# Loading k in runs of four rows and turning all of q by DMA in a fused attention and feed-forward kernel

## The chip, the cores and the metric

The kernel runs on one core of one Trainium2 chip. The metric is the device time of one execution in microseconds; of the kernel before there are three runs. Engines are named as the profile names them: PE is TensorE (its weight loads are PEld), DVE is VectorE, ACT is ScalarE, POOL is GpSimd, and SP is SyncE, which here only issues DMAs.

## The reference

Eight batches of eight heads attend in a sliding window of 64 tokens; the result, with the heads side by side, goes through a feed-forward layer whose activation is h cos h.

```
q, k, v: (8, 8, 576, 64) float32     w_in: (512, 2048)     w_out: (2048, 512)

scores = (q @ k^T) / 8
mask   = (0 <= pos_q - pos_k < 64);   scores = where(mask, scores, -1e9)
attn   = softmax(scores)
x      = (attn @ v) as (8*576, 512)
h      = x @ w_in;   g = h * cos(h);   out = g @ w_out
```

## The kernel before

Everything that PE multiplies is bf16. The feed-forward part goes over nine tiles (mt) of 512 tokens. The first tile is written out by hand as a list of short names (FIRST), with the attention of batches 0 and 1. Each later tile has a first product (h_ps, 16 blocks of 128 columns of w_in, four matmuls each) and a second product (out_ps, four groups of 16 matmuls). After each of the 16 blocks ACT makes the sine (L595) and DVE multiplies it with h_ps into gT (L598), which frees the PSUM bank; h_ps takes turns in five banks. The second product reads all of gT.

The attention of the later batches is laid into these tiles by a plan: `at(time, fn, ...)` puts a step on it, and `pump(time)`, called after each block of the first product and after every four matmuls of the second, emits all steps that are due. One unit of this time is four matmuls of 512 columns, some 0.9 us; a tile has T = 32 units. The plan sets only the order in which instructions stand in each engine's queue. An engine takes its queue in order and waits at each instruction for what that one needs; an engine with nothing to wait for runs ahead of the plan.

Batch b is prepared in tile b - 1, which starts at t0 = T (b - 1):

- POOL issues the loads, which cast to bf16. `load_chunk` brings 96 tokens of all heads of q or k (six chunks each), `load_v` brings v.
- `turn_k` (L260) has SP issue a DMA transpose of each k chunk into kT, six per batch. `turn_q` (L244) does the same with q chunks into one tile `turned`, for as many chunks as TURNED tells: two in batches 4 to 6, six in batch 7. They are put on the plan about 6 to 9 units ahead of t0.
- The other q chunks are transposed on PE (`tr_q`, L219) and copied out of PSUM by DVE. From `turned` DVE copies as well (`put_turned`). Both write `qB`, in which each unit of 64 tokens stands as a block of 128 columns, one half for each head of a pair, zero elsewhere; so one matmul gives the scores of two heads.
- `g_scores` (L303) multiplies each unit with the keys of its own and the preceding 64 tokens (in the order that alternates from unit to unit). The groups of a batch start at t0 + 14.6, so just as the second product starts, and follow at 0.36 units per unit of work.
- `g_max` (DVE) adds the mask and finds the maximum, `g_exp` (ACT) takes exponentials and their sum, `g_inv` (DVE) the reciprocal, `g_norm` (POOL, L353) multiplies into w, and `g_trans` (SP, L367) has w turned by a DMA transpose into wT.
- `values` (L384) multiplies wT with v into the next tile's x, just ahead of that tile.

Stores of a tile's output are issued by SP too (L473), at the next tile's start.

Of the kernel before, what the change touches and what calls it, by code (L numbers as in the profile page):

```python
# [10 lines left out]
def _safe_warn(msg, *a, **kw):  # L11
# [3 lines left out]
F32 = mybir.dt.float32  # L15
BF16 = mybir.dt.bfloat16
# [7 lines left out]
NU = 9  # L24
# [18 lines left out]
DIRECT = (0, 7, 8)  # L43
OUTS = 3
FILL = (6, 12)
TURNED = {4: 2, 5: 2, 6: 2, 7: 6}

# [24 lines left out]
)  # L72


# [1 line left out]
def kernel(  # L76
# [59 lines left out]
    def copy(engine, out, in_):  # L136
        {"a": nc.scalar.copy, "p": nc.gpsimd.tensor_copy}.get(engine, nc.vector.tensor_copy)(out, in_)  # L137
# [17 lines left out]
            nc.scalar.copy(mask16[:, lo:hi], mask[:, of:of + hi - lo])  # L155


    def rows_tile(name):
        return ld.tile([128, NC * H * D], BF16, tag=name, name=name)

    def load_heads(name, b, p0=0, n=PAIRS):
        if (name, b) not in st:
# [90 lines left out]
    def k_tile(b):  # L253
        if ("kA", b) not in st:
            st["kA", b] = ka = att.tile([128, PAIRS, S], BF16, tag="kT", name="kT", bufs=2)
            st.update({("kT", b, p): ka[:, p] for p in range(PAIRS)})
        return st["kA", b]

    def turn_k(b, c):
        nc.sync.dma_start(out=k_tile(b)[:, :, c * NP:c * NP + NP], in_=st["k", b][:, c], transpose=True)  # L260

    def put_k(b, p, engine="a"):
        kt = k_tile(b)[:, p]
# [18 lines left out]
    def g_scores(n, which):  # L282
        s_ps = bank((BANKS if n < n_listed else S_BANKS)[which], "s_ps")
        units = groups[n]
        if n == FILL[1]:
            nc.tensor.matmul(out=s_ps, lhsT=ident, rhs=mask16[:, 0:4].rearrange("p u c -> p (u c)"), start=True, stop=True,
                             skip_group_check=True)
        s_ps = s_ps[:, 0:len(units) * 128].rearrange("p (u c) -> p u c", c=128)
        if n < n_first:
            m0 = 2 if units[0][2] else 0  # L290
            for h in range(2):
                d = slice(64 * h, 64 * h + 64)
                nc.tensor.matmul(out=s_ps[d].rearrange("p u c -> p (u c)"), lhsT=ident[d, d],
                                 rhs=mask16[d, m0:m0 + len(units)].rearrange("p u c -> p (u c)"),
                                 start=True, stop=False, skip_group_check=True)
        for u, (b, p, j) in enumerate(units):
            kt = st["kT", b, p]
# [4 lines left out]
            if b > 1:  # L302
                nc.tensor.matmul(out=s_ps[:, u, 0:64 * chunks].rearrange("p (a t) -> p a t", a=chunks),  # L303
                                 lhsT=qblocks[(b % 2) * PAIRS + p][:, j].rearrange("d h t -> d (h t)"), rhs=rhs,
                                 start=True, stop=True, skip_group_check=True)
                continue
            for h in range(2):
                d = slice(64 * h, 64 * h + 64)
                nc.tensor.matmul(out=s_ps[d, u, 0:64 * chunks].rearrange("p (a t) -> p a t", a=chunks),  # L309
                                 lhsT=qtiles[b * PAIRS + p][d, 64 * j:64 * j + 64], rhs=rhs[d], start=n >= n_first,  # L310
                                 stop=n >= n_first or u == len(units) - 1, skip_group_check=True)
        st["s", n] = s_ps


    def g_max(n):
        s_ps, units = st["s", n], groups[n]
        negm = att.tile([128, GF], F32, tag="negm", name="negm", bufs=8)
        if n < n_first:
            nc.vector.tensor_reduce(out=negm[:, 0:len(units)], in_=s_ps, op=ALU.max, axis=AX.X, negate=True)
        else:  # L320
            s = att.tile([128, GF, 128], F32, tag="s", name="s", bufs=4)
            for u, (b, p, j) in enumerate(units):
                c = slice(0, 128 if j else 64)
                nc.vector.tensor_tensor_reduce(out=s[:, u, c], in0=s_ps[:, u, c], in1=mask[:, 2 - j % 2 if j else 0, c],  # L324
                                               scale=-scale if b else -1.0, scalar=BIG, op0=ALU.add, op1=ALU.min,
                                               accum_out=negm[:, u:u + 1])
            st["s", n] = s
        st["m", n] = negm
# [11 lines left out]
    def g_inv(n):  # L340
        e, den = st["e", n]
        for u, (_, _, j) in enumerate(groups[n]):
            if j == 0 and n >= n_first:
                nc.vector.memset(e[:, u, 64:128], 0.0)
        rden = att.tile([128, GF], F32, tag="rden", name="rden", bufs=8)
        nc.vector.reciprocal(out=rden[:, 0:len(groups[n])], in_=den[:, 0:len(groups[n])])  # L346
        st["r", n] = rden

    def g_norm(n, engine="p"):
        (e, _), rden = st.pop(("e", n)), st.pop(("r", n))  # L350
        w = att.tile([128, GF, 128], BF16, tag="w", name="w", bufs=8)
        u = len(groups[n])
        (nc.gpsimd if engine == "p" else nc.vector).tensor_tensor(out=w[:, 0:u], in0=e[:, 0:u], op=ALU.mult,  # L353
                                in1=rden[:, 0:u].unsqueeze(2).to_broadcast([128, u, 128]))
        st["w", n] = w

    def g_trans(n):
# [119 lines left out]
    def at(time, fn, *args):  # L477
        plan.append((time, len(plan), fn, args))
# [11 lines left out]
    for t in range(1, B - 1):  # L490
        last = max(i for i, units in enumerate(groups) if units[0][0] == t + 1)
        time = T * t + Q - 1.4
        for i in range(last + 1 - n):
# [9 lines left out]
            ready.update({unit: time + (5.9 if n in direct else 8.5) for unit in groups[n]})  # L503
            n += 1

    for b in range(2, B):
        t0 = T * (b - 1)
        for h in range(2):
            if b in TURNED:
                at(t0 + 0.6 + 0.5 * h, put_turned, b, h, 0, 3)  # L510
            if TURNED.get(b, 0) > 2:
                at(t0 + (11 + h if TURNED[b] == NC else 10 + 0.5 * h), put_turned, b, h, 3, TURNED[b] * NP // 64)
        for c in range(TURNED.get(b, 0)):
            at(t0 - T + (24.3 if b == 4 else 23.4 if c < 2 else 26.4) + 0.01 * c, turn_q, b, c)
        for p in range(PAIRS if TURNED.get(b) != NC else 0):
# [12 lines left out]
        for half_ in range(2):  # L528
            at(t0 + ((24 if b == 3 else 22.2) + 0.1 * half_ if b > 2 else 10), spread_v, b, half_, "p" if b > 2 else "s")
# [18 lines left out]
    def spread_first(lo, hi):  # L548
# [6 lines left out]
             "Lv0": lambda c: load_v(0, c), "Lv1": lambda c: load_v(1, c), "Lq2": lambda c: load_chunk("q", 2, c), "Lk2": lambda c: load_chunk("k", 2, c),  # L555
# [93 lines left out]
```

## Time and profile before

| | |
|---|---|
| time, median of 3 runs | 309.44 us (308.31 to 310.33) |
| span of the profiled execution, first to last instruction | 306.3 us; the page gives no other time of this execution |
| PE busy | 296.2 us, 97% of the span |
| PEld, DVE, ACT, POOL busy | 52%, 75%, 76%, 63% |
| granted clock of PE | 1.000 |
| DMA moved | 42.14 MB in 159,945 packets, 148,256 of them under 512 bytes |
| POOL's DMA queue | 100,192 packets, 18.06 MB |
| queue of SP | 59,568 packets, 23.38 MB |
| DMA transposes issued by SP | 68 of wT, 36 of kT, 12 of qT |

Busy times are sums over one profiled execution and may overlap between engines. Matmuls are pipelined, so that PE's busy time holds time in which its pipe fills; how far apart two matmuls start tells what one costs. A line of the profile's tables gives the source line, the engine and the operation, output and inputs by the program's names, how often, busy time and the mean time of one, and the idle time before it with what ended it. A timeline gives start, duration, engine, line and operation, with the idle time before in brackets. For SP the time of an instruction is the time to issue a DMA, not to move its data; that is listed as "to landing", from the issue on.

### The profile page before, as it was taken

To read this page: it belongs to the slowest core of one execution; us is meant where nothing else is said; L and a number is where in the kernel's file an instruction comes from. 1 tells how busy PE (TensorE), PEld (TensorE's weight loads), DVE (VectorE), ACT (ScalarE), POOL (GpSimd) and SP (SyncE) were. 2 spreads that over 40 slices of the span, in tenths; PEclk is the share of its full clock that TensorE was granted. 3 is DMA by queue.
4 is the path that set the end of the run, shared out by engine and by line. 5 is a ranking of instruction groups with operands and counts; after the bars stand their busy time and mean duration, and the time that the engine had idled before them with its cause. 6 is when DMAs were issued, how large, how long until landed. Compare 5 with 4: busy or idle time off the path is not lost.

```text
span 306.3 us, 7904 instructions
## 1 busy us (share of the span) xinstructions
PE 296.2 (97%) x2616; PEld 159.0 (52%) x2616; DVE 228.5 (75%) x908; ACT 234.3 (76%) x785; POOL 192.5 (63%) x228
## 2 busy tenths in 40 slices
PE   3889999999999999999999999999999999999996
PEld 2768844545555555445544555454545554454443
DVE  5999978599769976798579857986698668235801
ACT  5998799677997799779976997699879986116600
POOL 8998579995659669967998599959903930000000
PEclk9999999999999999999999999999999999999999
DMA  7999999999999995999999999999794643011011
GB/s 146 179 212 192 200 180 130 121 149 191 226 113 116 175 223 80 121 133 232 125 121 137 231 143 104 157 221 148 86 137 107 169 78 141 2 68 71 1 67 70
DMA packets 159945, 42.14 MB, mean 138 GB/s; under 512 B 148256, under 2 KB 155168, under 8 KB 159904
## 3 DMA queue, kind: packets, MB, share of 16 engines
q0 software_dynamic: 100192, 18.06, 80.1%
q1 hardware_dynamic: 59568, 23.38, 40.6%
q8 instruction: 20, 0.33, 0.4%
q14 instruction: 21, 0.17, 0.2%
q10 hardware_dynamic: 144, 0.20, 0.2%
HBM read 36.70 MB, written 9.44 MB: 151 GB/s over the span
## 4 chain that ended last, share of the span: by engine, by line
PE 90%; POOL 4%; DMA 2%; DVE 1%; ACT 1%; issue 1%; POOLq 0%; DVEq 0%; ACTq 0%
PE h_ps L453 35%; PE out_ps L609 35%; PE h_ps L417 5%; PE s_ps L303 4%; PE out_ps L436 4%; PE o_ps L384 3%; DMA k<-in_k_dram 2%; POOL w L353 2%; PE tq_ps L219 1%; POOL v L188 1%; PE out_ps L465 1%; PE s_ps L309 1%; PE tw_ps L364 1%; POOL w_in L204 1%; ACT e L336 1%
## 5 line engine op out<-in xcount | busy, mean ns | idle before, releaser
L609 PE MATMUL out_ps<-w_out,gT 128*128 128x512 bf16 x496 | 117.3, 379 | 0.0
L453 PE MATMUL h_ps<-xT,w_in 128*128 128x512 bf16 x512 | 115.3, 379 | 0.3
L595 ACT ACTIVATE sin<-h_ps 128x512 f32<-128x512 f32 x128 | 73.7, 598 | 32.7 <-PE h_ps L453 31.4
L598 DVE TENSOR_TENSOR gT<-h_ps,sin 128x512 bf16<-128x512 f32 x128 | 82.1, 685 | 21.9 <-ACT sin L595 21.2
L336 ACT ACTIVATE e<-s,negm 128x128 f32<-128x128 f32 (+1 forms) x256 | 97.1, 382 | 0.6 <-DVE negm L324 0.6
L353 POOL TENSOR_TENSOR w<-e,rden 128x512 bf16<-128x512 f32 (+1 forms) x74 | 70.0, 962 | 36.6 <-DVE rden L346 18.8
L453 PEld LDWEIGHTS <-w_in 128*128 128x128 bf16 x512 | 48.8, 98 | 54.7 <-issue 0.4
L609 PEld LDWEIGHTS <-gT 128*128 128x128 bf16 x496 | 45.9, 98 | 44.2
L324 DVE CUSTOM_DVE_ANT_0 s<-s_ps,mask 128x128 f32<-128x128 f32 (+1 forms) x256 | 56.4, 279 | 1.7 <-PE s_ps L309 0.9
L336 ACT ACTIVATION_READ_ACCUMULATOR e<-s,negm 128x1 f32 x256 | 48.3, 189 | 0.0
L182 POOL DMA_DIRECT2D q<-in_q_dram x36 | 28.3, 785 | 10.7 <-DMA q<-in_q_dram 4.0
L188 POOL DMA_DIRECT2D v<-in_v_dram x40 | 34.4, 878 | 0.3 <-issue 0.2
L182 POOL DMA_DIRECT2D k<-in_k_dram x36 | 28.2, 783 | 3.9 <-DMA k<-in_k_dram 1.2
L137 ACT COPY out_sb<-out_ps 128x512 f32<-128x512 f32 (+1 forms) x18 | 10.2, 566 | 24.5 <-PE out_ps L609 18.4
L346 DVE RECIPROCAL rden<-den 128x4 f32<-128x4 f32 (+1 forms) x79 | 13.1, 166 | 19.0 <-ACT e L336 18.6
L303 PEld LDWEIGHTS <-qB 128*128 128x128 bf16 x216 | 16.5, 98 | 14.2
L137 DVE CAST xT<-o_ps 128x512 bf16<-128x512 f32 x24 | 15.5, 677 | 10.1 <-PE o_ps L384 10.1
L137 DVE COPY out_sb<-out_ps 128x512 f32<-128x512 f32 x18 | 12.4, 690 | 13.2 <-PE out_ps L609 12.5
L324 DVE DVE_READ_ACCUMULATOR2_ANT negm<- 128x1 f32 x256 | 21.3, 83 | 0.0
L303 PE MATMUL s_ps<-kT,qB 128*128 128x128 bf16 (+1 forms) x216 | 21.2, 216 | 0.0
L137 POOL COPY v<-v 64x1536 bf16<-64x1536 bf16 (+3 forms) x12 | 18.8, 1570 | 0.3
L137 DVE COPY qB<-tq_ps 64x384 bf16<-64x384 bf16 (+1 forms) x40 | 15.6, 390 | 0.4
(70 smaller groups left out, 257.8 us busy)
## 6 DMA issues: line engine op xcount, KB each, us to landing
out_dram<-out_sb SPq DMA_DIRECT2D x16, 512.0 KB, 7.5
v<-in_v_dram POOLq DMA_DIRECT2D x32, 128.0 KB, 5.7
q<-in_q_dram POOLq DMA_DIRECT2D x36, 96.0 KB, 8.6
k<-in_k_dram POOLq DMA_DIRECT2D x36, 96.0 KB, 8.5
w_in<-in_moe_w_in_dram POOLq DMA_DIRECT2D x4, 512.0 KB, 8.7
w_out<-in_moe_w_out_dram POOLq DMA_DIRECT2D x4, 512.0 KB, 10.8
wT<-w SPq DMA_TRANSPOSE x68, 4.4
q<-in_q_dram POOLq DMA_DIRECT2D x7, 144.0 KB, 6.0
```

Of the source, the lines that this page charges most:

```text
L137: {"a": nc.scalar.copy, "p": nc.gpsimd.tensor_copy}.get(engine, nc.vector.tensor_copy)(out, in_)
L182: nc.gpsimd.dma_start(out=st[name, b][:, c].rearrange("p (h d) -> p h d", h=H), in_=src.rearrange("h p d -> p h d"))
L188: nc.gpsimd.dma_start(out=vt.rearrange("p (h d) -> p h d", h=H), in_=v[b, :, c * 128:c * 128 + n, :].rearrange("h p d -> p h d"))
L303: nc.tensor.matmul(out=s_ps[:, u, 0:64 * chunks].rearrange("p (a t) -> p a t", a=chunks), lhsT=qblocks[(b % 2) * PAIRS + p][:, j].rearrang ...
L324: nc.vector.tensor_tensor_reduce(out=s[:, u, c], in0=s_ps[:, u, c], in1=mask[:, 2 - j % 2 if j else 0, c], scale=-scale if b else -1.0, sc ...
L336: nc.scalar.activation(e[:, u, c], s[:, u, c], AF.Exp, bias=negm[:, u:u + 1], scale=1.0 if n < n_first else -1.0, accum_out=den[:, u:u + 1])
L353: (nc.gpsimd if engine == "p" else nc.vector).tensor_tensor(out=w[:, 0:u], in0=e[:, 0:u], op=ALU.mult, in1=rden[:, 0:u].unsqueeze(2).to_br ...
L417: nc.tensor.matmul(out=h_ps[:, half * e:half * e + half], lhsT=w_in_sb[:, ks, ff * 128:ff * 128 + 128], rhs=st["xT", 0][:, ks, half * g:ha ...
L453: nc.tensor.matmul(out=st["h", ff], lhsT=w_in_sb[:, ks, ff * 128:ff * 128 + 128], rhs=st["xT", mt][:, ks], start=start, stop=stop)
L595: nc.scalar.activation(sin, h_ps, AF.Sin, bias=math.pi / 2.0)
L598: nc.vector.tensor_tensor(out=gt[:, e], in0=h_ps, in1=sin, op=ALU.mult)
L609: nc.tensor.matmul(out=o_ps[e], lhsT=gT[ff // 2][:, ff % 2, ms * 128:ms * 128 + 128], rhs=w_out_sb[:, ff], start=ff == 0, stop=ff == n_ff - 1)
```

## The change

k of batches 2 to 7 is loaded in one DMA for the first 512 tokens, with each partition holding four consecutive tokens of every head (runs of 1 KB), and one for the last 64 (`load_runs`, `load_rest`). DVE sorts the first into an order in which token 4p + c stands in part c at row p (`sort_runs`), and two DMA transposes, of 16 blocks and of four, make kT of it (`turn_runs`, `turn_rest`). So keys stand in kT by their place in the run of four, and the score matmuls read them in pieces of 16 columns (`keys_of`); a ninth unit needs two matmuls. The mask is sorted alike once, and `g_norm` brings the weights back into the order of v: it reads e in the sorted order and writes every fourth element. The reciprocal is written twice for this.

q of batches 3 to 7 is turned by DMA whole. Its transposes are put on the plan at t0 + 1.6 to t0 + 6.6, the copies into blocks at t0 + 6, 6.5, 11 and 12. They stand behind the two stores in SP's queue. `load_v` follows from batch 3 on at t0 + 8, as it did for batch 7.

```diff
-TURNED = {4: 2, 5: 2, 6: 2, 7: 6}
+TURNED = {3: 6, 4: 6, 5: 6, 6: 6, 7: 6}
+RUN = 4
...
+    def sort_masks():
+        for to in range(2):
+            copy("d", mask[:, to].rearrange("q (a c p) -> q a c p", a=2, c=RUN),
+                 mask[:, to + 1].rearrange("q (a p c) -> q a c p", a=2, c=RUN))
...
+    def load_runs(b, lo, hi):
+        if ("raw", b) not in st:
+            st["raw", b] = rows_tile("k")[:, 0:RUN * H * D].rearrange("p (h x) -> p h x", h=H)
+        nc.gpsimd.dma_start(out=st["raw", b][:, lo:hi],
+                            in_=k[b, lo:hi, 0:128 * RUN].rearrange("h (p c) d -> p h (c d)", c=RUN))
+
+    def load_rest(b):
+        st["rest", b] = rest = ld.tile([64, H * D], BF16, tag="rest", name="rest", bufs=1)
+        nc.gpsimd.dma_start(out=rest.rearrange("p (h d) -> p h d", h=H),
+                            in_=k[b, :, 128 * RUN:S].rearrange("h p d -> p h d"))
+
+    def sort_runs(b, engine=None):
+        st["sorted", b] = to = ld.tile([128, RUN * H * D], BF16, tag="sorted", name="sorted", bufs=1)
+        copy(engine, to.rearrange("p (c h d) -> p h c d", c=RUN, h=H),
+             st.pop(("raw", b)).rearrange("p h (c d) -> p h c d", c=RUN))
...
-    def turn_k(b, c):
-        nc.sync.dma_start(out=k_tile(b)[:, :, c * NP:c * NP + NP], in_=st["k", b][:, c], transpose=True)
+    def runs_of(b):
+        whole = k_tile(b).rearrange("d a s -> d (a s)")
+        return (whole[:, 0:128 * RUN * PAIRS].rearrange("d (c a p) -> d c a p", c=RUN, a=PAIRS),
+                whole[:, 128 * RUN * PAIRS:].rearrange("d (a t) -> d a t", a=PAIRS))
+
+    def turn_runs(b):
+        nc.sync.dma_start(out=runs_of(b)[0].rearrange("d c a p -> d (c a) p"), in_=st.pop(("sorted", b)), transpose=True)
+
+    def turn_rest(b):
+        nc.sync.dma_start(out=runs_of(b)[1], in_=st.pop(("rest", b)), transpose=True)
+
+    def keys_of(b, p, j):
+        runs, rest = runs_of(b)
+        n = 64 // RUN
+        if j == NU - 1:
+            return ((0, 1, rest[:, p].rearrange("d (p c) -> d c p", c=RUN).unsqueeze(1)),
+                    (1, 2, runs[:, :, p, n * j - n:n * j].unsqueeze(1)))
+        lo, chunks = max(n * j - n, 0), 2 if j else 1
+        keys = runs[:, :, p, lo:lo + n * chunks].rearrange("d c (a p) -> d a c p", a=chunks)
+        return ((0, chunks, keys[:, ::-1] if j and j % 2 == 0 else keys),)
...
+            multiply(out=w[:, 0:u].rearrange("q u (a p c) -> q (u a) c p", a=2, c=RUN),
+                     in0=e[:, 0:u].rearrange("q u (a c p) -> q (u a) c p", a=2, c=RUN), op=ALU.mult,
...
+    at(T + 4, sort_masks)
     for b in range(2, B):
         t0 = T * (b - 1)
-        for h in range(2):
-            if b in TURNED:
-                at(t0 + 0.6 + 0.5 * h, put_turned, b, h, 0, 3)
-            if TURNED.get(b, 0) > 2:
-                at(t0 + (11 + h if TURNED[b] == NC else 10 + 0.5 * h), put_turned, b, h, 3, TURNED[b] * NP // 64)
-        for c in range(TURNED.get(b, 0)):
-            at(t0 - T + (24.3 if b == 4 else 23.4 if c < 2 else 26.4) + 0.01 * c, turn_q, b, c)
+        if b in TURNED:
+            for c in range(NC):
+                at(t0 + 1.6 + c, turn_q, b, c)
+            for h in range(2):
+                at(t0 + 6 + 0.5 * h, put_turned, b, h, 0, 3)
+                at(t0 + 11 + h, put_turned, b, h, 3, NU)
...
         if b > 2:
+            at(t0 - T + 5.6, load_runs, b, 0, H)
+            at(t0 - T + 6.4, load_rest, b)
             for c in range(NC):
-                for i, name in enumerate(("q", "k")):
-                    at(t0 - T + 5.6 + 1.6 * c + 0.8 * i, load_chunk, name, b, c)
-        for c in range(NC):
-            at(t0 + (2 + 1.2 * c if b == 2 else (-5.4, -5.3, -5.2, -4, -2.5, -1.5)[c] if TURNED.get(b) == NC else c - 5.5),
-               turn_k, b, c)
+                at(t0 - T + 7.2 + 1.6 * c, load_chunk, "q", b, c)
+        at(t0 + (1.4 if b == 2 else -9.4), sort_runs, b)
+        at(t0 + (2 if b == 2 else -6.5), turn_runs, b)
+        at(t0 + (3.2 if b == 2 else -5.5), turn_rest, b)
```

More of the change, by code (lines that the diff above doesn't have):

```diff
@@ L296, in g_scores @@
         for u, (b, p, j) in enumerate(units):
+            if b > 1:
+                for a0, a1, keys in keys_of(b, p, j):
+                    nc.tensor.matmul(out=s_ps[:, u, 64 * a0:64 * a1].rearrange("p (a c t) -> p a c t", a=a1 - a0, c=RUN),
+                                     lhsT=qblocks[(b % 2) * PAIRS + p][:, j].rearrange("d h t -> d (h t)"), rhs=keys,
+                                     start=True, stop=True, skip_group_check=True)
+                continue
             kt = st["kT", b, p]
@@ L301, in g_scores @@
                 rhs = rhs[:, ::-1, :]
[L302 to L306, printed above, removed]
             for h in range(2):
@@ L323, in g_max @@
                 c = slice(0, 128 if j else 64)
-                nc.vector.tensor_tensor_reduce(out=s[:, u, c], in0=s_ps[:, u, c], in1=mask[:, 2 - j % 2 if j else 0, c],
+                nc.vector.tensor_tensor_reduce(out=s[:, u, c], in0=s_ps[:, u, c], in1=mask[:, 1 - j % 2 if b > 1 else 2 - j % 2 if j else 0, c],
                                                scale=-scale if b else -1.0, scalar=BIG, op0=ALU.add, op1=ALU.min,
@@ L344, in g_inv @@
                 nc.vector.memset(e[:, u, 64:128], 0.0)
-        rden = att.tile([128, GF], F32, tag="rden", name="rden", bufs=8)
-        nc.vector.reciprocal(out=rden[:, 0:len(groups[n])], in_=den[:, 0:len(groups[n])])
+        rden = att.tile([128, GF, 2], F32, tag="rden", name="rden", bufs=8)
+        u, twice = len(groups[n]), 2 if n >= n_listed else 1
+        nc.vector.reciprocal(out=rden[:, 0:u, 0:twice], in_=den[:, 0:u].unsqueeze(2).to_broadcast([128, u, twice]))
         st["r", n] = rden
@@ L352, in g_norm @@
         u = len(groups[n])
-        (nc.gpsimd if engine == "p" else nc.vector).tensor_tensor(out=w[:, 0:u], in0=e[:, 0:u], op=ALU.mult,
-                                in1=rden[:, 0:u].unsqueeze(2).to_broadcast([128, u, 128]))
+        multiply = (nc.gpsimd if engine == "p" else nc.vector).tensor_tensor
+        if n < n_listed:
+            multiply(out=w[:, 0:u], in0=e[:, 0:u], op=ALU.mult, in1=rden[:, 0:u, 0:1].to_broadcast([128, u, 128]))
+        else:
+            multiply(out=w[:, 0:u].rearrange("q u (a p c) -> q (u a) c p", a=2, c=RUN),
+                     in0=e[:, 0:u].rearrange("q u (a c p) -> q (u a) c p", a=2, c=RUN), op=ALU.mult,
+                     in1=rden[:, 0:u].rearrange("q u a -> q (u a)").unsqueeze(2).unsqueeze(3)
+                     .to_broadcast([128, 2 * u, RUN, 64 // RUN]))
         st["w", n] = w
@@ L504 @@
             n += 1
+    at(T + 4, sort_masks)
     for b in range(2, B):
         t0 = T * (b - 1)
[L508 to L515 removed]
+        if b in TURNED:
[4 more added lines that the diff above has]
+                at(t0 + 11 + h, put_turned, b, h, 3, NU)
+        for p in range(PAIRS if b not in TURNED else 0):
             t_q = t0 + (2 if b == 2 else 1) + (3.3 if b == 2 else 3.5) * p
```

4 lines of the change are left out of this document (2 added, 2 removed), and 6 rows, old and new, of the table FIRST.

## The prediction, made before the run

> **What bounds the kernel now.** I read the page's chain of waits first, to see which engine sets the end.
>
> ```profile
> PE 90%; POOL 4%; DMA 2%; DVE 1%; ACT 1%; issue 1%; POOLq 0%; DVEq 0%; ACTq 0%
> ```
>
> TensorE (PE) holds 90% of the chain, and what is not PE lies almost wholly before 60 us. After that PE runs without a gap, so a microsecond of PE work taken away is a microsecond won, and a microsecond in which PE has to wait is one lost. The change does something to both, once per tile of 512 tokens. So I next read the chain in order of time for one such period. Call P the start of a tile's first product (h_ps, L453); its score matmuls (s_ps) and second product (out_ps, L609) follow. Here are tile 4, where batch 5 is prepared, and tile 6, where batch 7 is prepared:
>
> ```profile
> 152.76 2.75 PE h_ps L453 x12
> ...
> 167.63 1.73 PE out_ps L609 x8
> ```
> ```profile
> 215.85 13.97 PE h_ps L453 x64
> 229.82 0.20 PE s_ps L303 x4
> ```
>
> In tile 6 all of q is turned by DMA already, and the 64 matmuls take 13.97 us, unbroken. In tile 4 sixteen PE transposes of q lie between them: the second product begins at 167.63 instead of 14.2 us after P, 0.7 us later. These are what the change takes away.
>
> What it adds is work for SP's queue, which issues every DMA transpose in order. So the third view is SP's own timeline around P = 152.76, with GpSimd's (POOL's) last normalisation beside it:
>
> ```profile
> 150.70 3.81 SPq L367 DMA_TRANSPOSE wT<-w  x3
> 154.60 2.51 SPq L260 DMA_TRANSPOSE kT<-k  x2
> 157.21 1.21 SPq L367 DMA_TRANSPOSE wT<-w  x1
> 158.51 1.21 SPq L260 DMA_TRANSPOSE kT<-k  x1
> 159.82 1.24 SPq L367 DMA_TRANSPOSE wT<-w  x1
> 161.15 2.52 SPq L260 DMA_TRANSPOSE kT<-k  x2
> 163.78 1.28 SPq L367 DMA_TRANSPOSE wT<-w  x1
> 165.15 2.21 SPq L260 DMA_TRANSPOSE kT<-k  x1
> 167.47 1.06 SPq L473 DMA_DIRECT2D out_dram<-out_sb  x2
> ```
> ```profile
> 153.47 1.04 POOL L353 TENSOR_TENSOR w<-e,rden 128x512 bf16<-128x512 f32 x1 [0.55 <-DVE rden L346]
> ```
>
> The reader is to see a backlog. The last weights (w) are ready at 154.5, yet SP issues their transpose at 163.78 and the stores at 167.47, because every issue takes it 1.2 us, 1.3 with the gap, and twelve stand in line from 150.70 on. Today no urgent work stands behind this line: q of batch 5 went out in front of it (two chunks from 147.22), and all six of batch 7 too:
>
> ```profile
> 217.51 5.25 SPq L244 DMA_TRANSPOSE qT<-q  x4
> ```
> ```profile
> 227.65 0.54 DVE L137 COPY qB<-qT 64x1536 bf16<-64x1536 bf16 x1
> ```
>
> The last four are issued from P+1.7 to P+5.6 and land by P+11.2; VectorE (DVE) copies them into blocks at P+11.8, and the first score matmul follows at P+13.97. The slack is 0.6 us. The last view is the time from issue to landing, in traffic (kT, in tile 4) and in a quiet stretch (two chunks of q):
>
> ```profile
> L260 SPq DMA_TRANSPOSE kT<-k x6: 1207/1211/2215, 154.6 to 165.1; - x6
> ...
> DMA to landing us min/median/max: 3.7/6.9/8.2
> ```
> ```profile
> L244 SPq DMA_TRANSPOSE qT<-q x2: 1207/1207/1207, 117.5 to 118.8; - x2
> ...
> DMA to landing us min/median/max: 2.3/2.3/2.3
> ```
>
> **The change, part by part.** *PE transposes of q (L219) leave tiles 2 to 5.* From the first h_ps to the first out_ps these tiles take 14.99, 14.71, 14.71 and 14.70 us; tile 6, without transposes, 14.01. The differences add up to 1.0 + 3 x 0.7 = 3.1 us saved: 72 transposes at 43 ns.
>
> *Score matmuls.* The ninth unit of a head pair is now two of 64 columns: 24 more. A 64-column one occupies 28 ns in the trace, a 128-column one 56; two halves equal one whole, so between 0 and 24 x 28 ns = 0.7 us. I take 0.7. Keys are now read in runs of 16 columns with a jump, and the last 64 at every fourth column. No row shows such a read; the nearest are the units that read their two chunks in reverse order, which cost the same 56 ns. I take nothing; the other end is half speed, 216 x 52 ns = 11.3 us (3.7% of the span). The Trainium skill's SBUF — State Buffer (section on the DMA port swizzle) says that strides up to 8 bf16 elements are free, since two accesses still share a 16-byte line. By it this price is nothing and the sum stays; no run here shows it yet.
>
> *k in runs.* Per batch six loads of 256-byte rows become one of 1 KB rows and a small one; POOL loses four issues of 0.78 us, which the chain doesn't see. Sorting is one DVE copy per batch of 2048 values: from 0.54 us for 1536 up to 1.12 us (the 64x2048 copy of v), among scores in the second product, where DVE has pauses of 0.6 to 0.8 us waiting for ACT: hidden, at worst 6 x 1.1. DVE loses 32 copies of q out of PSUM (0.35 to 0.45 us) and gains ten of 0.37 and 0.55; it comes out lighter in the first product.
>
> *The sorted normalisation on POOL* writes every fourth element. No row shows that either; between today's 1.04 us and, at half speed, 2.1. It stands ahead of SP's backlog, which is longer, so I take no cost.
>
> *The two k transposes.* The issue of 16 blocks instead of 4: transposes of three and four blocks both take 1.2 us, so I take 1.3 with the gap; the other end is in proportion, 4.8, which is 3.6 us more per period. In tile 1 the big one stands ahead of the sixth group's wT, which landed just at its use; its 2048 packets of 28 ns over 16 engines delay it by 0 to 3.6 us: 2 once.
>
> *q behind the backlog, the step that decides.* All six chunks of batches 3 to 7 are now emitted behind the two stores. For tile 4: the fifth wT can go at 149.6, when its w is ready; then the sixth wT, the runs, wT, the rest, three wT: eight issues x 1.3 = 10.4; stores 1.2. So the first chunk goes at 161.2 = P+8.4, the sixth 6.5 later, at P+14.9. The same count gives P+14.9 for tiles 5 and 6. In tiles 2 and 3, where fewer wT stand behind, the last w is ready at P+1.5 and P+1.7 and the sixth chunk goes at P+12.7. To these comes the landing. POOL loads the next batch in this stretch (before: from 154.45 for 15 us, much the same now), so I take 7 us, by the kT row; in tile 6, where only v is loaded, 3. Ends: 2.3 and 8.2.
>
> Behind the copy of q on DVE are queued the products gT (L598), for which PE waits: they free the five banks of h_ps. And the score matmuls read the blocks themselves. From the first late copy to the first score matmul it was 229.82 - 227.65 = 2.2 us. So PE waits, per tile, for landing + 2.2 - 14.0:
>
> - tiles 2 and 3: 12.7 + 7 + 2.2 - 14 = 7.9 each
> - tiles 4 and 5: 14.9 + 7 + 2.2 - 14 = 10.1 each
> - tile 6: 14.9 + 3 + 2.2 - 14 = 6.1
>
> Together 42.1 us. The first copy, for units 0 to 2, waits as well, for chunks 0 and 1 (P+9.7 or earlier, + 7), but this wait ends before the other and lies inside it. It does not fade from tile to tile, as SP's line forms anew from the scores of each second product, which move with PE.
>
> **The sum.** 306.3 - 3.1 + 0.7 + 2 + 42.1 = 348.0 us of span. The runs' median, 309.44, lies 3.1 above the span of the profiled one, so the time is 351.
>
> **Rivals.** *Quiet landings.* If traffic is thin when q goes out (the k load moves fewer packets), every chunk lands in 2.3 us: 4 x 4.7 + 0.7 = 19.5 less, 331.5. For it: 2.3 us at 117 to 119. Against: all six kT of the loading stretch took 3.7 to 8.2. The Trainium skill's DMA: Bandwidth & Descriptors (section on the anatomy of one DMA) has a fit, made for DMAs that GpSimd issues, of 2.0 us plus bytes over 436 GB/s; it would make it 2.2 us, close to this rival's, and the loaded rows here contradict it. Chance 0.17.
>
> *A dearer tail.* The 16-block transpose holds SP for 4.8 us: 5 x 3.6 = 18 more, 369; or strided scores at half speed, 362. For it: issues of 2.0 to 2.2 us now and then; against: three blocks cost what four cost. Chance 0.16.
>
> *No wait at all (the other side).* If the sixth chunk lands by P+11.8, the copy finds it and only the saving is left: 306.3 - 3.1 + 0.7 + 3.1 = 307.0. That needs the first chunk out by P+3.0 with a quiet landing, 5.4 us earlier than I count in tile 4. For it: four k transposes fewer stand ahead of the stores in every period. Against: even with none, the last w is ready at P+1.7, and its wT (1.3) and the stores (1.2) put the first chunk at P+4.2. Chance 0.12.
>
> **How the numbers follow.** Forecast 0.55 (its own range 337 to 363: landings of 4 to 8.2 us, with the ends of the wT in tile 1). Range 325 to 376: from below the quiet rival to past the dear tail. A measurement here tells about 1% from no change. The rival of the other side lies 0.8% under the old time, so its 0.12 splits evenly: faster 0.06, same 0.06; all else, 0.88, is slower.
>
> **What would show it.** SP's timeline: six qT in a row behind two stores, the first 6 to 8 us after P. PE idle 6 to 10 us in each of tiles 2 to 6, in two stretches, and not in tiles 1, 7 and 8; DVE idle before copies of q, with the DMA of qT as releaser. L219 down to 24 instructions. A first product of 14 us in tiles 2 to 6 would prove me wrong; so would qT issued before P+3; if s_ps shows more than 56 ns from start to start, it was the strided read.

## The result, and the profile after

The changed kernel takes 375.6 us (median of four runs, 374.1 to 377.7) against 309.2 for the kernel before: a ratio of 1.214, with a 95% interval of 1.208 to 1.219. It is slower, by 66 us. The profiled execution took 374.1 us with a span of 372.2; all comparisons of parts below are made against the span of 306.3 before. Ratios and medians leave out executions that ran over 1.5% above the fastest of their kernel, and of e8_q_ahead_two_rests the profile is of such a slow one (338.6 us).

The chain of waits is read first again. Where PE held 90% of it, it now holds 58%:

```profile
PE 58%; DMA 18%; SPq 7%; POOL 7%; DVE 4%; issue 3%; ACT 2%; DVEq 0%; POOLq 0%; ACTq 0%
```

Who waits for whom is in the table of waits (engine, line, releaser; then the total in us, the number of waits and the longest):

```profile
DVE qB L138 <- DMA qT<-q: 63.3, 10, 13.6
...
PE h_ps L502 <- DVE gT L648: 45.6, 6, 11.7
...
POOL rest L199 <- DMA kT<-rest: 33.2, 5, 11.4
```

The first line is VectorE waiting for the turned q, twice in each of five tiles. The second is PE waiting for the products gT that stand behind those copies. The third is a wait on GpSimd, which comes up again below.

One tile shows the order of events. These are SP's queue, DVE's copies of q, and PE, in tile 4, whose first product starts at P = 179.54 (start, length, engine and line, what, count; in brackets the idle time before and what ended it):

```profile
167.88 11.65 SPq L416 DMA_TRANSPOSE wT<-w  x6
179.63 3.09 SPq L287 DMA_TRANSPOSE kT<-sorted  x1
182.83 1.21 SPq L416 DMA_TRANSPOSE wT<-w  x1
184.13 1.50 SPq L290 DMA_TRANSPOSE kT<-rest  x1
185.73 3.82 SPq L416 DMA_TRANSPOSE wT<-w  x3
189.65 1.05 SPq L522 DMA_DIRECT2D out_dram<-out_sb  x2
190.79 9.71 SPq L266 DMA_TRANSPOSE qT<-q  x6
```
```profile
200.73 0.35 DVE L138 COPY qB<-qT 64x768 bf16<-64x768 bf16 x1 [13.63 <-DMA qT<-q]
...
206.64 0.55 DVE L138 COPY qB<-qT 64x1536 bf16<-64x1536 bf16 x1 [2.06 <-DMA qT<-q]
```
```profile
179.54 10.52 PE L502 MATMUL h_ps<-xT,w_in 128*128 128x512 bf16 x48
201.74 5.34 PE L502 MATMUL h_ps<-xT,w_in 128*128 128x512 bf16 x16 [11.67 <-DVE gT L648]
207.84 0.30 PE L340 MATMUL s_ps<-kT,qB 128*128 128x64 bf16 x3 [0.77 <-DVE gT L648]
```

q stands at the end of SP's line: the first chunk goes out at P+11.2, the sixth at P+19.7, and the last copy can start at P+27.1. PE has done 48 of its 64 matmuls by P+10.5, waits 11.7 us for gT, does the rest (5.3 us for 16, since the granted clock is 0.5 right after the wait), and reaches the scores at P+28.3 instead of P+14.5.

The same reading for every tile, in us after P (first product: from the first h_ps to the first out_ps):

| tile | first product before | after | sixth chunk out | landed | second product before | after |
|---|---|---|---|---|---|---|
| 1 | 15.31 | 16.28 | - | - | 16.84 | 21.16 |
| 2 | 14.99 | 23.80 | 15.4 | 22.3 | 16.90 | 17.52 |
| 3 | 14.70 | 26.39 | 17.0 | 24.3 | 16.84 | 16.97 |
| 4 | 14.71 | 28.96 | 19.7 | 27.0 | 16.84 | 16.97 |
| 5 | 14.70 | 28.83 | 19.4 | 26.8 | 16.84 | 16.97 |
| 6 | 14.01 | 23.70 | 19.2 | 21.5 | 16.84 | 16.98 |

The first products of tiles 7 and 8 are unchanged (13.81 each). Of the 65.9 us, 58.6 lie in the first products of tiles 2 to 6, and 5.3 in tile 1.

### The profile page after: what moved, and what is told of

The parts are those of the page before. It is cut to its first block, busy times and chain, and to the rows that moved or that the text cites. A ratio compares the mean times of both kernels' runs of the same rounds, so it can differ in the third digit from the quotient of the medians.

```text
span 372.2 us, 7757 instructions
## 1 busy us (share of the span) xinstructions
PE 309.9 (83%) x2568; PEld 160.0 (43%) x2568; DVE 227.8 (61%) x894; ACT 235.2 (63%) x785; POOL 185.2 (50%) x204
## 4 chain that ended last, share of the span: by engine, by line
PE 58%; DMA 18%; SPq 7%; POOL 7%; DVE 4%; issue 3%; ACT 2%; DVEq 0%; POOLq 0%; ACTq 0%
PE out_ps L659 26%; PE h_ps L502 17%; DMA qT<-q 8%; SPq L266 6%; DMA q<-in_q_dram 6%; PE h_ps L466 4%; PE s_ps L340 3%; PE out_ps L485 3%; DMA kT<-sorted 2%; PE o_ps L433 2%; DVE gT L648 2%; DMA kT<-rest 1%; POOL w L400 1%; POOL w L398 1%; DVE qB L138 1%
## 5 line engine op out<-in xcount | busy, mean ns | idle before, releaser
L502 PE MATMUL h_ps<-xT,w_in 128*128 128x512 bf16 x512 | 126.9, 410 | 45.9 <-DVE gT L648 45.6
L400 POOL TENSOR_TENSOR w<-e,rden 128x512 bf16<-128x512 f32 (+1 forms) x59 | 67.7, 1245 | 76.0 <-DVE rden L389 74.4
L502 PEld LDWEIGHTS <-w_in 128*128 128x128 bf16 x512 | 52.8, 104 | 115.3 <-issue 65.5
L648 DVE TENSOR_TENSOR gT<-h_ps,sin 128x512 bf16<-128x512 f32 x128 | 82.3, 685 | 24.5 <-ACT sin L645 24.0
L138 DVE COPY qB<-qT 64x768 bf16<-64x768 bf16 (+1 forms) x20 | 9.1, 454 | 63.6 <-DMA qT<-q 63.3
L138 ACT COPY out_sb<-out_ps 128x512 f32<-128x512 f32 (+1 forms) x18 | 10.2, 566 | 24.5 <-PE out_ps L659 18.4
L340 PEld LDWEIGHTS <-qB 128*128 128x128 bf16 x240 | 17.6, 98 | 17.6 <-issue 2.1
L340 PE MATMUL s_ps<-kT,qB 128*128 128x64 bf16 (+1 forms) x240 | 22.5, 216 | 1.9 <-DVE gT L648 0.8
L138 DVE CAST xT<-o_ps 128x512 bf16<-128x512 f32 x24 | 15.4, 674 | 13.8 <-PE o_ps L433 13.8
L389 DVE RECIPROCAL rden<-den 128x8 f32<-128x8 f32 (+3 forms) x79 | 14.1, 180 | 15.1 <-ACT e L378 14.9
L366 DVE DVE_READ_ACCUMULATOR2_ANT negm<- 128x1 f32 x256 | 21.2, 83 | 0.0
L199 POOL DMA_DIRECT2D rest<-in_k_dram x6 | 4.1, 686 | 33.2 <-DMA kT<-rest 33.2
```

Source lines behind the costliest of these rows:

```text
L340: nc.tensor.matmul(out=s_ps[:, u, 64 * a0:64 * a1].rearrange("p (a c t) -> p a c t", a=a1 - a0, c=RUN), lhsT=qblocks[(b % 2) * PAIRS + p][ ...
L400: multiply(out=w[:, 0:u].rearrange("q u (a p c) -> q (u a) c p", a=2, c=RUN), in0=e[:, 0:u].rearrange("q u (a c p) -> q (u a) c p", a=2, c ...
L502: nc.tensor.matmul(out=st["h", ff], lhsT=w_in_sb[:, ks, ff * 128:ff * 128 + 128], rhs=st["xT", mt][:, ks], start=start, stop=stop)
L648: nc.vector.tensor_tensor(out=gt[:, e], in0=h_ps, in1=sin, op=ALU.mult)
```

## The experiments

The theory: q's transposes stand behind SP's line, and each first product ends some 2 us after the sixth chunk has landed. The main rival: the loss comes from k in runs itself. For e3, e4, e6, e7 and e10 there is one time each; for the others a ratio with its interval.

### One part at a time

**e1_q_ahead**: only the place of q's transposes is undone.

```diff
-                at(t0 + 1.6 + c, turn_q, b, c)
+                at(t0 - T + (26 if b == 3 else 24.3 if b == 4 else 23.4) + 0.01 * c, turn_q, b, c)
```

> Only the place of q's transposes is undone: all six of each batch are emitted ahead of the last wT and of the stores. Theory (the late landing of q's sixth chunk, because q stands behind SP's line, is the loss): the sixth chunk lands before the first product's 14th us, VectorE's waits for the DMA of qT fall from 63 us to under 8, the first products of tiles 2 to 6 take 14.0 to 15.0 us each, and the time falls from 375 to 308 to 318; what is left over 307 is the wait for wT in tile 1 (4 us) and what the k transposes, now last in the line, may still make late. Rival (the runs of k themselves cost it: the strided keys, the spread normalisation on GpSimd, the transposes of 16 blocks that hold SP): the time stays at 350 or more.

Measured: 331.1 us, ratio to before 1.070 (1.065 to 1.075). DVE's waits for qT are gone from the table, and the sixth chunk lands at P+7.6 to P+10.5. So two thirds of the loss go with this one line, and the rival falls. But the time is above the 308 to 318 expected: the second products of tiles 3 to 5 take 20.6 to 21.9 us (17.0 in the changed kernel), and first products of up to 17.1 follow. The place of q hid a second loss.

**e2_k_alone**: k in runs, q turned as before.

```diff
-TURNED = {3: 6, 4: 6, 5: 6, 6: 6, 7: 6}
+TURNED = {4: 2, 5: 2, 6: 2, 7: 6}
...
-                at(t0 + 1.6 + c, turn_q, b, c)
...
+        for c in range(TURNED.get(b, 0)):
+            at(t0 - T + (24.3 if b == 4 else 23.4 if c < 2 else 26.4) + 0.01 * c, turn_q, b, c)
```

> k in runs as in the changed kernel, q exactly as before (16 or 48 of a batch's transposes on TensorE or ahead of the line, batch 7 by DMA at the old times). Theory (q's place is the loss): no late q, the first products of tiles 2 to 5 at 14.7 to 15.0 us as before, plus the wait for wT in tile 1 (4 to 5 us) and 0.7 us for the extra score matmuls: 311 to 318. Rival (k's runs are the loss): 350 or more. If the transposes of 16 blocks delay wT in every tile, the second products would grow from 16.8 to over 18 and the time would be near 320.

Measured: 321.6 us, ratio 1.037 (1.034 to 1.040): 12 us where 2 to 9 were expected. Tiles 3 to 5 are as before (14.7 and 17.0). In tile 1 the scores wait 2.9 us for the transpose of 16 blocks and the values 3.7 us for a wT issued behind the next one; tile 2 follows with 16.7 us at a granted clock of 0.90, and tile 6 with 16.5, where q of batch 7 now lands at P+14.6.

**e3_q_alone**: k in six chunk transposes as before, q all by DMA behind the stores.

```diff
-TURNED = {4: 2, 5: 2, 6: 2, 7: 6}
+TURNED = {3: 6, 4: 6, 5: 6, 6: 6, 7: 6}
...
+                at(t0 + 1.6 + c, turn_q, b, c)
```

> k as before (six chunk transposes per batch, chunks loaded as before), q of batches 3 to 7 all by DMA and emitted behind the stores as in the changed kernel. Theory (the place of the sixth chunk in SP's line sets the end of the first product): four more k transposes of 1.2 to 1.3 us stand ahead of q, less the 2 us or so by which a transpose of 16 blocks is dearer, so the sixth chunk goes out 2 to 4 us later, at 18 to 23 us after P; first products of 26 to 32 us in tiles 3 to 5, the time 375 to 395. Rival (k's runs are the loss, q's place is not): under 330.

Measured: 385.1 us. The sixth chunk goes out at P+21.2 to P+22.7 and lands at P+24.5 to P+27.9; the first products take 26.7 to 31.1 us. The longer line is the worse one. k in runs alone costs 12 us, but with q behind the line it saves some 9 (375.6 against one time of 385.1), because it shortens what q waits behind: the sixth chunk goes out 2.6 to 5.8 us earlier in tiles 2 to 6.

**e11_q_ahead_k_before**: k as before, q all by DMA and ahead of the line.

```diff
-TURNED = {4: 2, 5: 2, 6: 2, 7: 6}
+TURNED = {3: 6, 4: 6, 5: 6, 6: 6, 7: 6}
...
-            at(t0 - T + (24.3 if b == 4 else 23.4 if c < 2 else 26.4) + 0.01 * c, turn_q, b, c)
+            at(t0 - T + (26 if b == 3 else 24.3 if b == 4 else 23.4 if c < 2 else 26.4) + 0.01 * c, turn_q, b, c)
```

> The kernel before, with k in six chunk transposes, but q of batches 3 to 7 all turned by DMA and issued ahead of the last wT, as before does it for batch 7 alone. Theory (q's place was the loss, and the transposes of 16 blocks, which hold SP for 3 to 8 us in traffic, are what stays lost when q goes ahead): the first products of tiles 2 to 6 fall to 14.0 to 14.5 us, with second products of 16.8 to 18; 305 to 313 us, well under the 332 of e1_q_ahead. Rival (22 transposes of 1.3 us and two stores are 29.8 us of SP in a period of 31.5, so that all of q by DMA doesn't fit there in any form): waits for wT or kT of 2 to 5 us per tile, 317 to 335.

Measured: 322.1 us, ratio 1.042 (1.037 to 1.046). Here the rival holds: now k is late, because it stands behind q. PE's waits for it make 9.4 of the 14.5 us by which the span grew.

```profile
PE s_ps L303 <- DMA kT<-k: 9.4, 9, 1.9
```

So all of q by DMA costs 13 us even with k as before and q in front. **e12_four_ahead** asks how much room SP has: four chunks ahead in batches 4 to 6 instead of two (`TURNED = {4: 4, 5: 4, 6: 4, 7: 6}`, the kernel before otherwise).

> The kernel before with four chunks of q instead of two turned by DMA ahead of the line in batches 4 to 6 (k as before). Theory (PE sets the end, and SP has 4 to 5 us to spare per period): 8 transposes of 43 ns less per tile, 0.3 us in each of three tiles, so 307.5 to 309.5, 0.1 to 0.5% under the kernel before. Rival (SP's line has less room than its sum says): the two added chunks make k or wT late, 312 to 322.

Measured: 315.8 us, ratio 1.021 (1.018 to 1.024). Two more transposes per period already make kT late: PE waits 4.8 us for it, three times, in tiles 3 and 5. (Another 2.5 of the 7.7 us by which the span grew lie ahead of tile 1, which the edit doesn't touch; why is open. Without them it is 1.7%.) SP's timeline is one nearly unbroken line (no pause over 0.5 us) from the first wT of tile 3's second product, at 145.5, to the last store, at 175.9; idle are only the 4 us before it and the 2 us behind it.

### Where exactly PE waits

**e4_copies_late**: DVE's copies of q planned behind all products gT.

```diff
-                at(t0 + 6 + 0.5 * h, put_turned, b, h, 0, 3)
-                at(t0 + 11 + h, put_turned, b, h, 3, NU)
+                at(t0 + 14.2 + 0.1 * h, put_turned, b, h, 0, 3)
+                at(t0 + 14.4 + 0.1 * h, put_turned, b, h, 3, NU)
```

> The changed kernel with VectorE's copies of q into blocks planned behind all its products gT, so that a late q holds no gT. Theory (the scores need the blocks, so the landing itself is what PE waits for): TensorE does all 64 matmuls of the first product first and then waits in one stretch; the first product still ends 2 to 3 us after the sixth chunk has landed; 368 to 378 us. Rival (the copies block VectorE's queue and gT behind them is the loss): PE waits only for what is left after its 14 us, with the loss cut by more than a third, under 355 us.

Measured: 378.8 us. PE now does its 64 matmuls in one piece (62 of them are in the trace of tile 4) and waits afterwards, for the copies:

```profile
183.09 13.97 PE L502 MATMUL h_ps<-xT,w_in 128*128 128x512 bf16 x62
204.63 0.45 PE L340 MATMUL s_ps<-kT,qB 128*128 128x64 bf16 x3 [7.56 <-DVE qB L138]
210.56 0.29 PE L340 MATMUL s_ps<-kT,qB 128*128 128x128 bf16 x1 [5.48 <-DVE qB L138]
```

The first products of tiles 2 to 6 are 7.6 us shorter in all and the second 9.9 us longer, since the low clock after the wait now falls on these (0.86 to 0.92 in the mean, 1.00 in the changed kernel). In tiles 3 to 6 the first product still ends 1.4 us after the sixth chunk has landed (2 to 3 expected). So the copies that block gT only decide where PE waits; how long is decided by the landing.

### The two sizes: landing and issue

**e6_thin_traffic** leaves out the loads of q for batches 4 to 7 and of v for batches 3 to 7.

```diff
-                at(t0 - T + 7.2 + 1.6 * c, load_chunk, "q", b, c)
+                if b == 3:
+                    at(t0 - T + 7.2 + 1.6 * c, load_chunk, "q", b, c)
+            if b > 3:
+                at(t0 - T + 7.2, lambda b: st.update({("q", b): st["q", b - 2]}), b)
...
-        for c in range(5):
+        for c in range(5 if b == 2 else 0):
```

> The changed kernel without the loads of q for batches 4 to 7 (older rows are turned instead) and without the loads of v for batches 3 to 7: it leaves these transfers out, every transpose and all arithmetic stay. Theory (transfers from memory lengthen both the issue and the landing of transposes): the sixth chunk lands 2.3 to 3.5 us after its issue instead of 7.3, issues of q take 1.3 us each instead of 1.5 to 1.8, the first products of tiles 3 to 5 shrink from 26 to 29 us to 19 to 23, and the time is 340 to 355. Rival (landings wait for the other transposes, not for loads): they stay at 6 us or more and the time at 365 or more.

Measured: 350.6 us. From issue to landing of q's 30 chunks (the last line; in the changed kernel it reads 2.3/7.2/9.8):

```profile
L266 SPq DMA_TRANSPOSE qT<-q x30: 1185/1256/2513, 99.0 to 267.5; - x30
...
DMA to landing us min/median/max: 2.3/2.4/6.9
```

In tiles 4 and 5 the sixth chunk still goes out at P+19.3 and P+18.7, but lands 2.4 us later instead of 7.3, and the first products take 24.0 and 23.9 us, 5.0 less than in the changed kernel but over the 19 to 23 expected. So these loads cost the landing 5 us; of SP's late issue they make only 0.4 to 0.8 us in tiles 4 to 6, and 2.3 and 1.5 in tiles 2 and 3. With the landing this early, PE's clock shows: in tile 3 the sixth chunk lands at P+17.9, but PE comes out of its wait for gT at P+16.3, needs 5.7 us for the last 16 matmuls (3.5 at full clock; 0.50 is granted until P+19.8), and only then reaches the scores.

**e10_k_early_q_late** takes the k transposes of batches 4 to 7 out of the line ahead of q.

```diff
-        at(t0 + (1.4 if b == 2 else -9.4), sort_runs, b)
-        at(t0 + (2 if b == 2 else -6.5), turn_runs, b)
-        at(t0 + (3.2 if b == 2 else -5.5), turn_rest, b)
+        at(t0 + (1.4 if b == 2 else -9.4 if b == 3 else 15.2 - T), sort_runs, b)
+        at(t0 + (2 if b == 2 else -6.5 if b == 3 else 16.2 - T), turn_runs, b)
+        at(t0 + (3.2 if b == 2 else -5.5 if b == 3 else 16.3 - T), turn_rest, b)
```

> The changed kernel with q where it was, behind the stores, and only the two k transposes of batches 4 to 7 taken out of the line ahead of q (to the start of the second product). Theory (each microsecond of SP's issuing ahead of q is a microsecond of the first product): the sixth chunk goes out 4 to 5 us earlier in tiles 3 to 6, where the two transposes held SP for 3.0 and 1.5 us; the first products of these tiles shrink by as much; 354 to 364 us. Rival (the landing in traffic, not the issue, sets it): the chunks land when they landed before, 368 to 378.

Measured: 364.3 us. The sixth chunk goes out 2.2 to 4.0 us earlier in tiles 3 to 6, and the first products are 2.0 to 4.5 us shorter. The direction is as expected, the size a little under it, and so the time just above its range.

### What q's place had hidden

In e1_q_ahead GpSimd waits 42.9 us for the one buffer of the last 64 rows of k, whose transpose stands late in SP's line; v, w and then wT come late.

```profile
POOL rest L199 <- DMA kT<-rest: 42.9, 4, 11.3
```

**e8_q_ahead_two_rests** gives e1_q_ahead a second buffer (`bufs=1` to `bufs=2` in load_rest).

> As e1_q_ahead, with two buffers for the last 64 rows of k instead of one. In e1_q_ahead the second products of tiles 3 to 5 take 20.6 to 21.9 us instead of 17.0, and GpSimd stands 11 to 13 us per period before the load of these rows, waiting for the transpose that reads them; its later loads, v's spread and the normalisations then come late. Theory (this wait of GpSimd is what is left): the waits for the rest buffer vanish, the second products of tiles 3 to 5 return to 17 to 18 us, the granted clock of the first products that follow rises from 0.85 to 0.90 to 1.0, and the time falls from 332 to 312 to 319. Rival (the last wT, which now stand behind six q transposes on SP, are what is late): the second products stay at 19 us or more and the time at 326 or more.

Measured: ratio 1.075 (1.065 to 1.085), so no better than e1_q_ahead: the theory falls, and its rival named the wrong transfer. GpSimd's wait is gone, and the loads it held back now start beside the transpose of 16 blocks. In the profiled execution (338.6 us) that one lands 13.2 and 12.6 us after its issue in tiles 3 and 4 (7.9 and 6.2 in e1_q_ahead), and the scores wait for it:

```profile
PE s_ps L340 <- DMA kT<-sorted: 18.5, 4, 5.1
```

**e7_two_rests** is the same edit on the changed kernel.

> The changed kernel with two buffers for the last 64 rows of k instead of one, nothing else. Theory (q's late landing hides GpSimd's wait for that buffer, 33 us in all): the wait vanishes and the time stays within 372 to 379, since the loads come earlier but the transposes of q stand where they stood. Rival (the blocked GpSimd, which makes the last w and so the line of wT late, sets the sixth chunk's issue): the sixth chunk goes out 2 us or more earlier in tiles 4 to 6 and the time falls to 362 or less.

Measured: 381.2 us, a little over the theory's range. The wait vanishes, the sixth chunk goes out at 15.6 to 21.3 us after P (15.4 to 19.7 without the edit), and tile 1 now waits 5.3 us for the transpose of 16 blocks: it lands after 14.4 us instead of 9.3, with the loads of q issued from 1.1 us after it on, while in the changed kernel they follow when it has landed. So the wait for this buffer had kept the loads off the transposes.

**e5_all_ahead** (e8_q_ahead_two_rests with the k transposes right behind q) and **e9_k_early** (e1_q_ahead with them behind the stores, at the start of the second product):

```diff
-        at(t0 + (2 if b == 2 else -6.5), turn_runs, b)
-        at(t0 + (3.2 if b == 2 else -5.5), turn_rest, b)
+        at(t0 + (2 if b == 2 else -5.9 if b == 3 else -7.5 if b == 4 else -8.5), turn_runs, b)
+        at(t0 + (3.2 if b == 2 else -5.8 if b == 3 else -7.4 if b == 4 else -8.4), turn_rest, b)
```
```diff
-        at(t0 + (1.4 if b == 2 else -9.4), sort_runs, b)
-        at(t0 + (2 if b == 2 else -6.5), turn_runs, b)
-        at(t0 + (3.2 if b == 2 else -5.5), turn_rest, b)
+        at(t0 + (1.4 if b == 2 else -9.4 if b == 3 else 15.2 - T), sort_runs, b)
+        at(t0 + (2 if b == 2 else -5.9 if b == 3 else 16.2 - T), turn_runs, b)
+        at(t0 + (3.2 if b == 2 else -5.8 if b == 3 else 16.3 - T), turn_rest, b)
```

> As e8_q_ahead_two_rests, with the two k transposes too placed ahead of the late wT, right behind q. Theory (in its old place the transpose of 16 blocks holds SP for 3 to 4 us just ahead of the last wT): 0 to 4 us better than e8_q_ahead_two_rests in tile 1 and in the second products; 308 to 316. Rival (SP's line is full there in any order, and what is put ahead only moves the lateness to wT): the same as e8_q_ahead_two_rests or 2 to 8 us more, with waits of PE for wT of over 2 us per tile.

> As e1_q_ahead (q ahead, one buffer for the rest), with the two k transposes of batches 4 to 7 a whole stretch earlier: behind the stores at the start of the second product, where SP stands idle for 5 us or more, and those of batch 3 behind the sixth wT. Theory (what e1_q_ahead still loses is k: GpSimd's wait for the rest buffer makes v, w and wT late, and the runs land late in traffic): both go, the second products of tiles 3 to 6 take 17.0 to 17.5 us, the first products 14.0 to 14.7; what is left is tile 1 (3 to 6 us) and tile 2 (0 to 4): 310 to 319. Rival (with q and k in runs SP has too little room in any order): second products of 19 us or more in tiles 3 to 6 and a time of 325 or more.

Measured: 1.061 (1.053 to 1.068) and 1.052 (1.037 to 1.066). Neither comes down to the times hoped for. e9_k_early does remove the long wait for wT at the end of tile 1 (1.0 us left of 4.0), and its second products in tiles 3 to 6 fall to 17.0 to 18.1; but in tile 2 the transpose of 16 blocks holds SP for 7.7 us, and wT comes 4.5 us late. Here is the same transpose, issued early in the second product of tile 3, in e9_k_early and in e10_k_early_q_late (a stretch of exactly one issue each, its length, the busy time of each engine with the number of instructions, the granted clock, the DMA share and GB/s):

```profile
150.82:156.08 5.26, 5.21 (x37) 2.84 (x37) 4.97 (x46) 5.26 (x30) 4.06 (x4) 1.00 1.63 254
```
```profile
165.10:167.15 2.05, 2.05 (x15) 1.03 (x13) 2.05 (x19) 2.05 (x12) 1.12 (x1) 1.00 0.43 85
```

Beside stores and loads (254 GB/s) it holds SP for 5.3 us; with its own data alone (85 GB/s) for 2.1. Over the four batches it is 5.3 to 7.7 us at 208 to 254 GB/s and 1.8 to 2.3 at 71 to 97. The total rate is not what sorts such issues, though: in the changed kernel one took 1.7 us at 127 GB/s and one 3.1 at 79. In the changed kernel and the nine experiments that have this transpose, it held SP for 1.7 to 3.7 us where GpSimd's queue (q0) moved nothing meanwhile (32 issues), and for 3.1 to 8.1 where it did (28). No version here beats the kernel before.

## Why the prediction was right, and which sizes were off

The forecast was 351 with a range of 325 to 376, slower, and its mechanism is the one that the runs show. The size is another matter: the forecast's own range, 337 to 363, was missed by 13 us, and 375.6 lies inside the wider one by luck, since two of the four runs (377.1 and 377.7) are above it. One term carries most of the difference.

- **Transposes off PE, 3.1 us: right.** L241 (before: L219) has 24 instructions left. Where nothing is late, the saving is there in full: tile 3 of e1_q_ahead takes 14.01 us (14.70 before), tile 2 of e9_k_early 13.97 (14.99). In the changed kernel it drowns in the wait.
- **Score matmuls, 0.7 us, and strided keys, nothing: right in the sum.** The second products grew by 0.13 us in tiles 3 to 6, which is 0.8 if all six batches pay it. A score matmul of 128 columns still takes 56 ns from start to start (median), and one of 64 columns in four runs of 16 still 28, so the other end of 11.3 us is out. But the two halves of a ninth unit take 41 ns (the one at every fourth column) and 49 (the one in runs), not 28 each: 90 instead of 56, which four times per batch is the 0.13. The rule of the Trainium skill's SBUF — State Buffer, quoted in the prediction, is not tested by this: only the half of 41 ns reads at such a stride, and since the other half is as slow, the stride need not be the reason. Which it is stays open.
- **Sorted normalisation on GpSimd: 1.37 us for 128x512**, within the bounds of 1.04 and 2.1. That it costs the end nothing was not separated from the rest of e2_k_alone.
- **The wT of tile 1, 2 us taken, 0 to 3.6 as ends: too small.** The values wait 4.0 us for it, the second product is 4.3 longer. With the transpose of 16 blocks put behind that wT (e9_k_early, which also moves q) 1.0 is left.
- **Landing, 7 and 3 us: right.** Measured 6.9 to 7.4 in tiles 2 to 5, and 2.3 in tile 6. The row of kT in traffic was the right one to take. The fit in the Trainium skill's DMA: Bandwidth & Descriptors (the anatomy of one DMA), by which a chunk is estimated at 2.2 us, agrees with the 2.4 of e6_thin_traffic and not with the 7.2 in traffic; so the rival of quiet landings had the right figure for the wrong stretch.
- **From the landing to the first out_ps, 2.2 us: right.** Measured 1.5 to 2.2.
- **The issue of the sixth chunk: the step that was mis-sized.** The prediction counted P+12.7, 12.7, 14.9, 14.9 and 14.9; measured were 15.4, 17.0, 19.7, 19.4 and 19.2, together 20.6 us later. In tile 4 the 4.8 us are made of three parts: the fifth wT went at P-2.5 instead of P-3.2 (0.7); from it to the stores the eight issues took 12.6 us instead of 10.4 (2.2), of which the transpose of 16 blocks alone makes 1.9 (3.09 us and the gap, against 1.3); and from the first to the sixth chunk of q it was 8.5 us instead of 6.5 (2.0), of which the first makes 1.6 (2.86 us and the gap). One price of 1.3 us was taken for every issue. The other transposes of three and four blocks nearly kept to it there (1.2 to 1.5 us), beside loads or not; the large one did not, nor did the first one behind the stores. While that one was issued, only the queue of SP (q1) moved data, at 308 GB/s, 430 of its 446 packets of 2 KB or more. Here are the stretch and its queue:

```profile
190.79:193.65 2.86, 0.00 (x0) 0.00 (x0) 0.00 (x0) 0.00 (x0) 2.78 (x5) 1.00 0.98 308
```
```profile
q1 hardware_dynamic: 446, 0.88, 97.7%
```

In e6_thin_traffic both stay dear in tile 4 (3.55 and 2.45 us), so the loads of q and v are not the reason there. That the stores' data are, for the first q, is the nearest reading; no run moves the stores alone. In tiles 2 and 3 the loads do make 2.3 and 1.5 us of the delay.

Put in, these give the span: 348.0 + 20.6 for the issues + 3.3 for tile 1 (4.3 and 1.0, less 2) = 371.9, against 372.2. What is left out nearly cancels: landings and what follows them are 1.0 less in all, and small growth elsewhere, most of it in tile 2's and tile 8's second products, is 1.4 more than the 0.7 taken.

Of the rivals, a dearer tail (369) was half true: the transpose of 16 blocks did hold SP longer, 3.0 us in the median and not 4.8; what no rival priced is the first q behind the stores. No wait at all (307.0) is refuted by the result itself, where the sixth chunk lands at P+21.5 or later; and e1_q_ahead and e11_q_ahead_k_before show that not even with q in front of the line did this split of the work reach the old time. The prediction did not see that, since its rival on the other side took the rest of SP's line as free.

## What to carry to other kernels

A queue that issues in order is a resource of its own: for each transfer put on it, count what stands ahead of it at the moment when it must go out, each issue at its own price (a large transpose, or one among other traffic, can cost several times a small one), and not from the sum over a period. A transfer that a compute engine waits for belongs ahead of those that only have to be done by the next period, but every place given to one is taken from another; here two more transposes per period already cost some 2%. When one wait is removed, look for what it was holding back: the wait for the rest buffer was also what kept the loads off the transposes.

## What was not expected of the hardware

**An issue has no fixed price.** In the changed kernel alone one transpose of 16 blocks holds SP for 1.7 to 6.0 us (both ends in tile 1), and for 7.7 in tile 2 of e9_k_early, where three or four blocks take 1.2 in most rows. The long ones fall together with GpSimd's loads; that they are due to them is read from these rows, not tested one by one.

**PE's clock after a wait.** In e1_q_ahead PE waits 1.4 and 2.7 us around 160 us, with four matmuls between; the granted clock (the column before the last two) is 0.50 until it has worked again for some microseconds:

```profile
162.00:164.35 2.35, 1.53 (x52) 1.47 (x53) 1.17 (x2) 0.39 (x2) 2.27 (x3) 0.50 0.42 73
164.35:166.00 1.65, 1.65 (x8) 0.58 (x5) 0.80 (x3) 1.55 (x2) 1.65 (x3) 0.50 0.44 92
166.00:168.00 2.00, 1.78 (x6) 0.79 (x6) 0.00 (x0) 0.00 (x0) 2.00 (x3) 0.66 0.26 50
168.00:170.00 2.00, 2.00 (x11) 0.94 (x10) 1.17 (x2) 1.80 (x4) 1.53 (x2) 1.00 0.33 65
```

The first product that begins at 164.35 has a mean clock of 0.90 and takes 15.50 us; 14.01 divided by 0.90 is 15.6. So a wait of 4 us at the end of a tile costs 1.5 us more in the next one. The Trainium skill's TensorE: Matmul & The Clock Gate (part 1, on the clock gate) tells of half the clock after an idle window of about 3.4 us, until one busy window has gone by; this trace agrees, with 0.50 up to 166 and 1.00 from 168, if the two waits count as one: each is under 3.4 us, and from the start of the first to the end of the second it is 4.3. In the changed kernel the clock is at 0.5 too, but there q's landing sets the end of the first product all the same, and the second products run at 1.00. In e4_copies_late and e6_thin_traffic it does cost time.

**GpSimd's writes.** Writing every fourth element with the factor read in pieces of 16 raised its 128x512 product from 1.04 to 1.37 us, by 31%, and the 128x384 one from 0.83 to 1.07. Which of the two costs it was not separated.
